# FNet plus MLP on one core: the MLP sums of row blocks 1 and 2 kept in bank layout and added in the last column transform

## The chip, the cores and the metric

The kernel runs on one core of a Trainium2 chip. The metric is device time in microseconds of one execution; for the kernel before it is 849.5 us, the median of three runs (849.11 to 849.95). The engines are named as in the profile: PE (TensorE, matmuls), PEld (its weight loads), DVE (VectorE), ACT (ScalarE), POOL (GpSimd) and SP (SyncE, which here only issues DMAs). An engine works through its own instructions in the order in which the program lists them, and waits for others by semaphores. "us" is microseconds. L189 means line 189 of the kernel before.

## What is computed

The input `x` has 2048 rows of 640 columns. With `xn` the rows of `x` normalised, the output is x plus the real part of a two-dimensional Fourier transform of `xn` plus a two-layer MLP of `xn` with a GELU between. Both parts are matrix products in float32:

```python
a = einsum("bsd,ed->bse", xn, dft_hid_re)
b = einsum("bsd,ed->bse", xn, dft_hid_im)
y = einsum("ts,bse->bte", dft_seq_re, a) - einsum("ts,bse->bte", dft_seq_im, b)
h = gelu(einsum("bsd,df->bsf", xn, w1) + b1)
out = x + y + einsum("bsf,fd->bsd", h, w2) + b2
```

## The kernel before

Each float32 operand of a matmul is split into a high and a low part (`split`, L176): ACT writes the high part (`high`, L186), DVE subtracts it from the operand for the low part (`low`, L189). A product is then three matmuls (`product`, L297 to L302): high by high, high by low, low by high. The rows are worked in four blocks `t` = 0 to 3 of 512 rows (`TB`). PE's results gather in eight PSUM banks of 128 partitions by 512 columns. The 640 output columns of a block are five column blocks `e` of 128. A bank holds one of them "as the matmul leaves it": 128 partitions of columns by 512 rows. To get to the row layout of `x` and of the output, DVE turns 32 by 32 blocks (`nc.vector.transpose`).

**The MLP first.** Its hidden products and output products run over the four row blocks; `oacc[t][e]` is the bank of the sum of block `t` and column block `e`. Block 0 comes first. The calls of `pair(k)` (L1059) then make the hidden units of blocks 1 and 2 together, and the output products of block 1. The last output products of block 1 and those of block 2 run in a loop over `p` = 0 to 13, where one step of PE is 15 matmuls or 3.4 us up to p = 11, with `between(p)` (L1107) as the work beside it. When the sum of a block is complete, each of its five banks is emptied: ACT adds the bias `b2c` in the bank, DVE transposes the bank into an SBUF tile, and DVE adds this to rows of `x` that were loaded for it (`load_xo`, L373). For block 1 these are `turn_sum` and `add_sum` at p = 1 and 4 and `finish` (L953) at p = 4, 5 and 6; for block 2 it is the function `fill` at p = 13. `store_sums` (L973) then writes x plus sum to DRAM, to the three tensors `ys`, split by columns (`YCOLS`: 64, 64 and 32 of the 160 columns that a group of 32 partitions holds). The SBUF tiles in which the transposes land are slots of rings of two: tags `yt`, `ab` and `zt`. The same `zt` slots are used at p = 7 to 9 by the transposes of the normalised rows of block 3 (`transpose_z`, L257). Those rows come by `put_z` (L778), sixteen DMAs issued half on POOL and half on SP at p = 3. `split_unit(g + 2, ...)` at step p prepares the operand `hs` which PE uses in step p + 2.

**The Fourier part after it.** The sequence transform runs first for one half (h = 0) and all four blocks, then for the other (h = 1), block 3 first. Behind blocks 3 and 0 stands one column transform for both (`("y", (3, 0))`), and behind blocks 1 and 2 the last one of the kernel. In it `ta` is 1 and `tb` is 2, and `last` is true. Each of these stages is a scheme of seven products `w` = 0 to 6 in place of eight. In a column transform each product has three entries `u`, so that the last stage has entries n = 0 to 20. `hidden_entry` (L1690) issues an entry's matmuls. They add into the banks named X, Y, Z (two banks each, so one bank past the first is `X + 1`), US and VS; the pairs are taken in the order X, Y, Z, X, Z, X, X for the seven products. The moving operand `as` is a ring of three tiles: behind entry n the kernel makes the operand of entry n + 3 (`form`, L547), with a `high` on ACT and a `low` on DVE, and then runs the work listed for n in `hidden_beside` (L1533, table at L1632). This table is the order in which DVE gets its work in the last stage. `t2`, `t3` and `t4` in it combine the sums `u` and `v` of the two blocks. The rest takes results out of the banks: `to` turns a bank pair and adds it to rows, `odd` does that for the bank US, `copy` moves a bank pair to a sum in SBUF with ACT, `v1` adds the bank pair X to the sum "v1", and `in_two` and `late_rows` turn such sums and add them to rows. `last_columns` turns 32 of each group's columns of block 1's rows into a tile `A["end"]`, and `end(k)` adds that to the last bank.

In the last stage the rows to which everything is added are block 1's `ya = yo[ta]`, loaded by `load_yo` (L1478), and block 2's `columns(0)`, `columns(1)` and `yo[tb, 4]`, loaded by `load_yb` (L1558) and `load_y4` (L1486). Before the change all of these hold x plus the MLP sum, from `ys`. Entry 18 issues fifteen matmuls into VS and fifteen into the first bank of X; entry 19 finishes the two halves of the second bank. After that DVE turns the last results and SP and ACT issue the stores.

Of the kernel before, what the change touches and what calls it, by code (L numbers as in the profile page):

```python
# [15 lines left out]
P = 128  # L16
# [10 lines left out]
def kernel(  # L27
# [72 lines left out]

    YCOLS = ((0, 2 * B), (2 * B, 4 * B), (4 * B, 5 * B))
    ys = [dram.tile([NT, P, NB, c1 - c0], F32, name=f"ys{k}") for k, (c0, c1) in enumerate(YCOLS)]

    GWIDE = (3, 3, 3, 2, 2, 2, 3)
    wits = [dram.tile([ND, P, 2, n * P], F32, name=f"wit{w}") for w, n in enumerate(GWIDE)]
# [867 lines left out]
    def store_sums(t, *ks):  # L973
        for k in ks or range(len(YCOLS)):
            c0, c1 = YCOLS[k]
            nc.gpsimd.dma_start(ys[k][t], xo[t][:, :, c0:c1])

    in_zt = {"home": mr, "tag": "zt"}

    LASTK = NF // 2 - 1  # L980

    def beside_pair(k, at):

        if k == 0:
# [36 lines left out]
        if k == 1:  # L1021
            steps = {7: (0,), 4: (1,)}
        elif k == 2:
            steps = {5: (-1,), 7: (0, 1), 4: (2,)}
        elif k == LASTK:
            steps = {3: (0,), 7: (1, 2)}
        else:
            steps = {3: (0,), 7: (1,), 4: (2,)}
        if at == (7 if k == 1 else 3) and j + 1 < ND:
            load_w(0, j + 1)  # L1030
            load_w(1, j + 1)
        if k == LASTK and at == 3:
            load_x(12)
            load_x(13)
        for n in steps.get(at, ()):
            prep_w(*((j - 1, 2) if n < 0 else (j, n)))
        if k == LASTK and at == 7:
            A["gs"] = place("xab3", (P, 5, TB), F32)
            for i in range(3, 6):
                load_unit(i)  # L1040
        if k == LASTK and at == 2:
            for i in range(3):
                load_unit(i)
        if k == LASTK and at == 4:
            load_x(14)
            load_x(15)
            for i in range(6, 8):
                load_unit(i)
            load_xo(1, place("xab2", (P, NB, DQ), F32))

    units = {}

# [54 lines left out]
    def between(p):  # L1107
# [2 lines left out]
            ln_stats(12)  # L1110
            ln_stats(13)
        if p == 1:
            held = [turn_sum(1, e) for e in (3, 4)]
            A["held"] = held
            ln_stats(14)
        if p == 2:
            ln_stats(15)
        if p == 3:
# [3 lines left out]
                ln_apply(c)  # L1122
            put_z(Z["z"], row_places, nc.gpsimd, nc.sync)
            new_xt(3)
        if p == 4:
            for e, yt in zip((3, 4), A["held"]):
                add_sum(1, e, yt)
        if 4 <= p < 7:
            finish(1, p - 4, home=in_zt)
        for j in {7: (0,), 8: (1, 2), 9: (3, 4)}.get(p, ()):  # L1130
            if j == 0:
                transpose_z("x30", Z["z"], 0)
# [10 lines left out]
        if p in (0, 1, 4, 8):  # L1143
            load_unit({0: 8, 1: 9, 4: 10, 8: 11}[p])
        if p == 10:
            store_sums(1)
            put_rows(3, row_places, nc.sync)
        if p == 12:
            load_xo(2)

    def fourier_step(i):
        if 2 <= i < 2 + 2 * NK:
# [54 lines left out]
    for p in range(2 + NF):  # L1207
# [4 lines left out]
        elif p == NF + 1:  # L1212
# [2 lines left out]

            def fill(k):
                if k == 0:
                    kept[3] = turn_sum(2, 3, rows, "yt")
                else:
                    kept[4] = turn_sum(2, 4, rows, "yt")  # L1220
                    kept[0] = turn_sum(2, 0, **in_zt)
                    kept[1] = turn_sum(2, 1, **in_zt)
                    kept[2] = turn_sum(2, 2)

            kept = {}
            gelu(g + 2, acc, fill)
            for e in (3, 4, 0, 1, 2):
                add_sum(2, e, kept[e])
            store_sums(2)
# [117 lines left out]
    PARTS = slice(0, TB // 2), slice(TB // 2, TB)  # L1347
    X, Y, Z, US, VS = 0, 3, 5, 2, 7
    yo = {}

    def beside(h, t, n):

# [107 lines left out]
        else:  # L1460
# [15 lines left out]
            if n == 6 and p == 2:  # L1476

                def load_yo():  # L1478
                    yo[t] = out_pool.tile([P, NB, DQ], F32, tag="zo", bufs=1, name=f"yo{t}")
                    for k, (c0, c1) in enumerate(YCOLS):  # L1480
                        nc.sync.dma_start(yo[t][:, :, c0:c1], ys[k][t])

                post.append(load_yo)
            if n == 6 and second:

                def load_y4():  # L1486
                    yo[t, 4] = A["y4"](f"y4_{t}")
                    nc.sync.dma_start(yo[t, 4], ys[2][t])

                post.append(load_y4)  # L1490
            if n == 11 and p == 3:
                post += [lambda: open_g(b), lambda: [load_g(b, i) for i in range(3, len(A["g", b]))]]
            if n == 13 and p == 1:
                post += [lambda: open_g(b), lambda: [load_g(b, i) for i in range(3, len(A["g", b]))]]
            if n == 13 and direct:
# [37 lines left out]
    def hidden_beside(b, n):  # L1533
# [22 lines left out]
            return s(1 if last else 0, ("u1", "u2")[k]).rearrange("p a b -> p (a b)").rearrange("p (n e) -> p n e", n=NB)  # L1556

        def load_yb(k):  # L1558
            return lambda: nc.sync.dma_start(columns(k), ys[k][tb])

        def copy(dst, src):
# [50 lines left out]
        def late_rows(h):  # L1612
# [77 lines left out]
    def hidden_entry(n, b, w, u):  # L1690
# [12 lines left out]
        if w == 6 and last:  # L1703

            if u == 0:
                for pos in range(ND):
                    use_g(bank(VS), 2, pos, False, pos == ND - 1)
                for pos in range(ND):
                    wide(0, pos)
            elif u == 1:  # L1710
# [10 lines left out]
        for pos in mine:  # L1721
            if w < 2:
                use_g(bank(US), 2, pos, w == 0 and pos == 0, w == 1 and pos == ND - 1)
            if w == 2:
                use_g(bank(VS), 2, pos, pos == 0, False)
            if w == 6 and u == 2:
                use_g(bank(VS), 2, pos, False, True)
        for pos in mine:
# [78 lines left out]
```

## The time and the profile before

| | |
|---|---|
| median of three runs | 849.5 us |
| lowest and highest run | 849.11 and 849.95 us |
| the profiled execution: first to last instruction (span) | 847.6 us |
| granted TensorE clock, mean | 1.00 |
| the last column transform, first to last matmul | 781.9 to 843.5 us |

The profiled execution gives its span only; the runs' times hold some 2 us more than that span, for what lies before the first and behind the last instruction. The rows of the profile read as follows. A timeline row has the start in us, the length in us, the engine, the line, the operation, what it writes and reads, and in brackets how long the engine was idle ahead of it and what ended that idle time. A row of stretches has, for PE, PEld, DVE, ACT and POOL in turn, the busy us and in parentheses the number of instructions, then the granted clock, the share of time in which the DMA engines were busy, and GB/s. A row of DMA issues has what is written from what, the queue, how many, the size of each, and the median us from issue to landing.

### The profile page before, as it was taken

How to read it: one execution, taken by the hardware profiler on the slowest of the kernel's cores; microseconds unless marked ns; L12 is line 12 of the kernel's file. 1: busy time of each engine (PE TensorE's matmuls, PEld its weight loads, DVE VectorE, ACT ScalarE, POOL GpSimd, SP SyncE). 2: the span in 40 equal slices, each digit the busy share in tenths (PEclk: the TensorE clock that was granted, in tenths of full speed). 3: DMA queues.
4: the chain of work that ended last, by engine and by line, in shares of the span. 5: the costliest groups of instructions: out<-in, count | busy, mean ns of one | idle time of the engine just before them, and what ended most of it. 6: DMA issues, size and time to landing. Idle time of an engine off the chain costs nothing.

```text
span 847.6 us, 10644 instructions
## 1 busy us (share of the span) xinstructions
PE 841.1 (99%) x3725; PEld 696.8 (82%) x3725; DVE 684.3 (81%) x902; ACT 366.1 (43%) x526; POOL 77.8 (9%) x135
## 2 busy tenths in 40 slices
PE   8999999999999999999999999999999999999998
PEld 7888888888888888888888888888888888888886
DVE  5969888767854778979978887899977998886687
ACT  6556657545453555443444343232322433223241
POOL 3340024222301000000000000000000000000012
PEclk9999999999999999999999999999999999999999
DMA  7995767878977897958644679663744799805454
GB/s 223 289 247 160 162 169 244 260 224 299 255 190 205 328 330 143 204 127 188 158 137 108 166 221 287 162 141 99 207 161 152 234 234 230 313 19 180 125 168 111
DMA packets 195332, 166.52 MB, mean 196 GB/s; under 512 B 57648, under 2 KB 166704, under 8 KB 194768
## 3 DMA queue, kind: packets, MB, share of 16 engines
q1 hardware_dynamic: 185216, 139.51, 61.7%
q0 software_dynamic: 7888, 25.83, 9.0%
q10 hardware_dynamic: 2176, 0.52, 0.3%
q8 instruction: 29, 0.48, 0.2%
q14 instruction: 23, 0.19, 0.1%
HBM read 115.75 MB, written 46.14 MB: 191 GB/s over the span
## 4 chain that ended last, share of the span: by engine, by line
PE 99%; ACT 0%; DMA 0%; issue 0%; DVE 0%; SPq 0%
PE banks L302 30%; PE banks L301 30%; PE banks L300 30%; PE banks L320 10%; DMA row<-in_A_x_dram 0%; PE banks L688 0%; ACT xp L721 0%; ACT scratch L715 0%; ACT xp L709 0%; ACT scratch L708 0%; DVE yo L1768 0%; SPq L208 0%; PE banks L742 0%; ACT mv L698 0%
## 5 line engine op out<-in xcount | busy, mean ns | idle before, releaser
L300 PE MATMUL banks<-as,xab 128*128 128x512 f32 (+1 forms) x412 | 159.4, 387 | 0.0
L302 PE MATMUL banks<-as,xab 128*128 128x512 f32 (+1 forms) x412 | 159.4, 387 | 0.0
L301 PE MATMUL banks<-as,xab 128*128 128x512 f32 (+1 forms) x412 | 159.4, 387 | 0.0
L186 ACT ACTIVATE as<-r 128x1024 fp32r<-128x1024 f32 x80 | 85.0, 1062 | 171.2 <-PE banks L302 147.5
L189 DVE TENSOR_TENSOR as<-r,as 128x1024 fp32r<-128x1024 f32 x80 | 97.2, 1216 | 38.1 <-ACT as L186 37.9
L301 PEld LDWEIGHTS banks<-as,xab 128*128 128x128 f32 x412 | 77.4, 188 | 15.7
L300 PEld LDWEIGHTS banks<-as,xab 128*128 128x128 f32 x412 | 77.4, 188 | 15.7
L302 PEld LDWEIGHTS banks<-as,xab 128*128 128x128 f32 x412 | 77.4, 188 | 15.7
L302 PE MATMUL banks<-as,xc 128*128 128x512 f32 x224 | 87.2, 389 | 0.0
L300 PE MATMUL banks<-as,xc 128*128 128x512 f32 x224 | 87.2, 389 | 0.0
L301 PE MATMUL banks<-as,xc 128*128 128x512 f32 x224 | 87.2, 389 | 0.0
L186 ACT ACTIVATE as<-rt 128x1024 fp32r<-128x1024 f32 x32 | 34.0, 1063 | 72.5 <-PE banks L302 57.9
L320 PE MATMUL banks<-xt,xab 128*128 128x512 f32 x240 | 56.7, 390 | 0.0
L320 PEld LDWEIGHTS banks<-xt,xab 128*128 128x128 f32 x240 | 45.0, 188 | 9.3
L1300 POOL DMA_DIRECT2D out_dram<-yo x4 | 2.6, 660 | 518.1 <-DVE yo L463 518.1
L189 DVE TENSOR_TENSOR hs<-ab,hs 128x512 fp32r<-128x512 f32 x36 | 24.7, 687 | 31.1 <-ACT hs L186 30.8
L302 PEld LDWEIGHTS banks<-as,xc 128*128 128x128 f32 x224 | 42.1, 188 | 8.8
L301 PEld LDWEIGHTS banks<-as,xc 128*128 128x128 f32 x224 | 42.1, 188 | 8.7
L300 PEld LDWEIGHTS banks<-as,xc 128*128 128x128 f32 x224 | 42.1, 188 | 8.7
L302 PE MATMUL banks<-hs,xc 128*128 128x512 f32 x120 | 46.7, 390 | 0.0
L300 PE MATMUL banks<-hs,xc 128*128 128x512 f32 x120 | 46.7, 390 | 0.0
L301 PE MATMUL banks<-hs,xc 128*128 128x512 f32 x120 | 46.7, 389 | 0.0
(240 smaller groups left out, 1684.2 us busy)
## 6 DMA issues: line engine op xcount, KB each, us to landing
raw<-in_A_dft_seq_re_dram SPq DMA_DIRECT2D x64, 256.0 KB, 5.5
raw<-in_A_dft_seq_im_dram SPq DMA_DIRECT2D x64, 256.0 KB, 5.0
w1r<-in_B_w_dram SPq DMA_DIRECT2D x144, 80.0 KB, 3.3
wit<-wst POOLq DMA_DIRECT2D x15, 384.0 KB, 4.1
wit<-wst POOLq DMA_DIRECT2D x20, 256.0 KB, 4.3
forms_ab<-xab SPq DMA_DIRECT2D x4, 1280.0 KB, 8.3
xab<-wit SPq DMA_DIRECT2D x13, 384.0 KB, 5.1
row<-xn SPq DMA_DIRECT2D x14, 320.0 KB, 7.0
```

What stands on the lines that cost most here:

```text
L186: nc.scalar.activation(h, s, AF.Copy)
L189: nc.vector.tensor_tensor(l, s, h.bitcast(F32), op=ALU.subtract)
L300: nc.tensor.matmul(acc, wh, mh, start=first, stop=False, skip_group_check=goes_on)
L301: nc.tensor.matmul(acc, wh, ml, start=False, stop=False, skip_group_check=goes_on)
L302: nc.tensor.matmul(acc, wl, mh, start=False, stop=last, skip_group_check=goes_on)
L320: nc.tensor.matmul(acc, W1[i][:, a, j * P : (j + 1) * P], XT[j][:, b], start=n == 0, stop=n == len(steps) - 1)
L1300: queues[q % len(queues)].dma_start(rows_of(out, t)[:, :, q * DQ + c0 : q * DQ + c1], src[q * B : (q + 1) * B])
```

## The change

The banks of blocks 1 and 2 are no longer turned and added to x. A new `keep_sum` adds the bias on ACT while it moves the bank to an SBUF slot, unturned, and POOL writes that to a DRAM tensor `sums_t[t]`. The loads of x rows in this part of the kernel (`load_xo(1)`, `load_xo(2)`), the transposes, the adds and `store_sums` for these blocks go. For block 0 `ys` stays as it was.

In the last stage the rows of blocks 1 and 2 are now loaded from `x` itself, in pieces of a group of 32 partitions each (`load_columns`, and `load_yo`). The kept sums are loaded by six POOL DMAs at the end of the last sequence transform (`load_sums`), into two places whose last use by PE is there. They are added in bank layout, by adds on DVE in the table of `hidden_beside`: to bank pair X on the way to SBUF at entry 3, the pair Y at entry 6, US for both blocks at entry 7, Z and X in place of two copies on ACT at entries 9 and 12, VS in place at entry 10, `A["end"]` at entry 11, and the first bank of X in place at entry 17. At entry 3 a transpose and an add go, since X and Y are turned together. The flags of PE's accumulation into VS change with the add into that bank; the matmuls are the same in number, shape and order.

```diff
+    sums_t = {t: dram.tile([P, ND, TB], F32, name=f"sums_t{t}") for t in (1, 2)}
...
+    def keep_sum(t, e, home=mr, tag="ab", name="ks"):
+
+        kept = home.tile([P, TB], F32, tag=tag, bufs=2, name=f"{name}{t}_{e}")
+        nc.scalar.activation(kept, oacc[t][e], AF.Identity, bias=b2c[:, e : e + 1])
+        nc.gpsimd.dma_start(sums_t[t][:, e], kept)
...
-            load_xo(1, place("xab2", (P, NB, DQ), F32))
...
         if p == 1:
-            held = [turn_sum(1, e) for e in (3, 4)]
-            A["held"] = held
+            for e in (3, 4):
+                keep_sum(1, e)
...
-        if p == 4:
-            for e, yt in zip((3, 4), A["held"]):
-                add_sum(1, e, yt)
         if 4 <= p < 7:
-            finish(1, p - 4, home=in_zt)
+            keep_sum(1, p - 4, **in_zt)
...
         if p == 10:
-            store_sums(1)
             put_rows(3, row_places, nc.sync)
-        if p == 12:
-            load_xo(2)
...
+    def load_columns(dst, t, c0, c1):
+        for q in range(Q):
+            nc.sync.dma_start(dst[q * B : (q + 1) * B], rows_of(x, t)[:, :, q * DQ + c0 : q * DQ + c1])
+
+    def load_sums(ta, tb):
+        a, b = (place(f"xc{n}{n + 1}", (P, 7, TB), F32) for n in (0, 2))
...
+        for dst, t, e0, e1 in ((a, ta, 0, 2), (a, ta, 4, 5), (b, tb, 4, 5), (b, tb, 2, 4), (b, tb, 0, 2), (a, ta, 2, 4)):
+            nc.gpsimd.dma_start(dst[:, e0:e1], sums_t[t][:, e0:e1])
...
+            if n == 13 and p == 3:
+                post.append(lambda: load_sums(blocks[b - 1][1], t))
...
         def load_yb(k):
+            if last:
+                return lambda: load_columns(columns(k), tb, *YCOLS[k])
...
+        sa, sb = A["sums"] if last else (None, None)
+        both = sa[:, 5:7] if last else None
+
+        def first_two():
+            add(both, both, y_)
+            to(ya[:, :, : 2 * B], both, f"ya2_{ta}", out_a(0, 2 * B))()
+
         def odd():
+            if last:
+                add(sa[:, 4], sa[:, 4], us)
+                add(sb[:, 4], sb[:, 4], us)
+                add_turned(ya[:, :, 4 * B :], turned(sa[:, 4], f"yo_{tb}"))
+                out_a(4 * B, DQ)()
+                return
...
-            3: [to(ya[:, :, : 2 * B], x_, f"ya1_{ta}")],
+            3: [lambda: add(both, x_, sa[:, 0:2])] if last else [to(ya[:, :, : 2 * B], x_, f"ya1_{ta}")],
...
-            6: [to(ya[:, :, : 2 * B], y_, f"ya2_{ta}", out_a(0, 2 * B)), t2(2)],
+            6: [first_two if last else to(ya[:, :, : 2 * B], y_, f"ya2_{ta}"), t2(2)],
...
-            9: [copy(s(1, "v1"), z_), t3(1)],
-            10: [t3(2)],
-            11: [t4(0)],
-            12: [copy(s(1, "v2"), x_), t4(1)],
+            9: [lambda: add(s(1, "v1"), z_, sb[:, 2:4]) if last else copy(s(1, "v1"), z_)(), t3(1)],
+            10: [t3(2)] + ([lambda: add(vs, vs, sb[:, 4])] if last else []),
+            11: [t4(0)] + ([lambda: add(A["end"], A["end"], sa[:, 3])] if last else []),
+            12: [lambda: add(s(1, "v2"), x_, sb[:, 0:2]) if last else copy(s(1, "v2"), x_)(), t4(1)],
...
-            17: [v1, *late_rows(0)] if last else [yb1, yb2],
+            17: [v1, lambda: add(bank(X), bank(X), sa[:, 2]), *late_rows(0)] if last else [yb1, yb2],
```

More of the change, by code (lines that the diff above doesn't have):

```diff
@@ L1217, in fill @@
                 if k == 0:
-                    kept[3] = turn_sum(2, 3, rows, "yt")
+                    keep_sum(2, 3, rows, "yt")
                 else:
[L1220 to L1225, printed above, removed]
+                    keep_sum(2, 4, rows, "yt")
+                    keep_sum(2, 0, **in_zt)
+                    keep_sum(2, 1, **in_zt)
+                    keep_sum(2, 2)
             gelu(g + 2, acc, fill)
-            for e in (3, 4, 0, 1, 2):
-                add_sum(2, e, kept[e])
-            store_sums(2)
         else:
@@ L1349 @@
     yo = {}
+    def load_columns(dst, t, c0, c1):
[3 more added lines that the diff above has]
+        a, b = (place(f"xc{n}{n + 1}", (P, 7, TB), F32) for n in (0, 2))
+        A["sums"] = a, b
+        for dst, t, e0, e1 in ((a, ta, 0, 2), (a, ta, 4, 5), (b, tb, 4, 5), (b, tb, 2, 4), (b, tb, 0, 2), (a, ta, 2, 4)):
+            nc.gpsimd.dma_start(dst[:, e0:e1], sums_t[t][:, e0:e1])
     def beside(h, t, n):
@@ L1479, in load_yo @@
                     yo[t] = out_pool.tile([P, NB, DQ], F32, tag="zo", bufs=1, name=f"yo{t}")
-                    for k, (c0, c1) in enumerate(YCOLS):
-                        nc.sync.dma_start(yo[t][:, :, c0:c1], ys[k][t])
+                    for q in range(Q):
+                        nc.sync.dma_start(yo[t][q * B : (q + 1) * B], rows_of(x, t)[:, :, q * DQ : (q + 1) * DQ])
                 post.append(load_yo)
@@ L1487, in load_y4 @@
                     yo[t, 4] = A["y4"](f"y4_{t}")
-                    nc.sync.dma_start(yo[t, 4], ys[2][t])
+                    if p == 3:
+                        load_columns(yo[t, 4], t, 4 * B, DQ)
+                    else:
+                        nc.sync.dma_start(yo[t, 4], ys[2][t])
                 post.append(load_y4)
@@ L1706, in hidden_entry @@
                 for pos in range(ND):
-                    use_g(bank(VS), 2, pos, False, pos == ND - 1)
+                    use_g(bank(VS), 2, pos, False, pos == ND - 1, True)
                 for pos in range(ND):
@@ L1724, in hidden_entry @@
             if w == 2:
-                use_g(bank(VS), 2, pos, pos == 0, False)
+                use_g(bank(VS), 2, pos, pos == 0, last and pos == ND - 1)
             if w == 6 and u == 2:
```

## The prediction

> **What bounds the kernel now.** I read the page's engine line first, then the table of who waited for whom with the rows of PE, then stretches of the last stage.
>
> ```profile
> span 847.6 us, 10644 instructions
> PE 841.1 (99%) x3725; PEld 696.8 (82%) x3725; DVE 684.3 (81%) x902; ACT 366.1 (43%) x526; POOL 77.8 (9%) x135
> ```
>
> ```profile
> PE banks L672 <- POOL warm L660: 2.0, 1, 2.0
> PE banks L688 <- ACT xp L721: 0.4, 1, 0.4
> ```
>
> TensorE (PE) is busy from end to end. Its only two waits in the whole span are before its first real product. The change neither adds nor removes a matmul, so in the body nothing can get shorter: work taken off VectorE (DVE), ScalarE (ACT) and the queues comes off engines for which PE never waits. The time can only grow, where an engine that now runs just ahead of PE falls behind it, or shrink in the few us after the last matmul. So the question is who has how much lead, and where the change puts its work. It puts it in the last stage, the column transform of row blocks 1 and 2 (781.9 to 843.5).
>
> ```profile
> 782.00:807.70 25.70, 25.70 (x115) 21.30 (x114) 14.65 (x15) 6.57 (x7) 0.00 (x0) 1.00 0.38 112
> 807.70:836.40 28.70, 28.70 (x128) 23.71 (x128) 27.40 (x29) 11.68 (x13) 5.18 (x8) 1.00 0.48 143
> 843.60:847.60 4.00, 0.00 (x0) 0.00 (x0) 0.40 (x1) 0.00 (x0) 0.00 (x0) 1.00 0.59 131
> ```
>
> These are stretches with the busy time of PE, PEld, DVE, ACT and POOL, then the granted clock. In the first 25.7 us DVE works 14.65; in the next 28.7 us it works 27.40. There it has 1.3 us to spare, and that is where six of the seven added operations land (the seventh, at entry 17, comes as that stretch ends). DVE's queue there, some rows left out:
>
> ```profile
> 807.73 1.23 DVE L189 TENSOR_TENSOR as<-u,as 128x1024 fp32r<-128x1024 f32 x1 [2.07 <-ACT as L186]
> 808.87 1.24 DVE L1322 STREAM_TRANSPOSE ya<-banks 128x1024 f32<-128x1024 f32 x1
> 810.15 1.23 DVE L463 TENSOR_TENSOR yo<-yo,ya 128x1024 f32<-128x1024 f32 x1
> ...
> 813.03 0.71 DVE L1319 STREAM_TRANSPOSE yo<-banks 128x512 f32<-128x512 f32 x1
> 813.77 0.69 DVE L463 TENSOR_TENSOR yo<-yo,yo 128x512 f32<-128x512 f32 x1
> 814.38 0.69 DVE L463 TENSOR_TENSOR y<-y,yo 128x512 f32<-128x512 f32 x1
> 814.98 0.68 DVE L189 TENSOR_TENSOR as<-u,as 128x512 fp32r<-128x512 f32 x1
> ...
> 816.72 1.22 DVE L189 TENSOR_TENSOR as<-v,as 128x1024 fp32r<-128x1024 f32 x1
> 817.86 1.22 DVE L463 TENSOR_TENSOR u<-u,u 128x1024 f32<-128x1024 f32 x1
> 819.98 1.23 DVE L189 TENSOR_TENSOR as<-v,as 128x1024 fp32r<-128x1024 f32 x1 [0.90 <-ACT as L186]
> ...
> 824.59 1.22 DVE L463 TENSOR_TENSOR v<-v,u 128x1024 f32<-128x1024 f32 x1
> 826.04 1.23 DVE L189 TENSOR_TENSOR as<-u,as 128x1024 fp32r<-128x1024 f32 x1 [0.23 <-ACT as L186]
> ...
> 828.39 1.22 DVE L463 TENSOR_TENSOR v<-v,banks 128x1024 f32<-128x1024 f32 x1
> 829.64 1.25 DVE L1322 STREAM_TRANSPOSE yb<-v 128x1024 f32<-128x1024 f32 x1
> ...
> 834.78 1.22 DVE L463 TENSOR_TENSOR v<-v,banks 128x1024 f32<-128x1024 f32 x1
> 836.03 0.71 DVE L1618 STREAM_TRANSPOSE yb<-v 128x512 f32<-128x512 f32 x1
> ```
>
> Read the start times. An operation of 1024 columns takes its successor 1.13 us later (816.72 to 817.86), one of 512 columns 0.60 (814.38 to 814.98), and a 1024 add whose result the next one reads 1.25 (828.39 to 829.64). From 807.73 to 836.03 the queue stops only at 819.98 and 826.04.
>
> **The prices, part by part.** I count places by the entries 0 to 20 of the stage (three to each of its seven products w; entries 18 to 20 are the last product).
>
> *Ahead of 807.73.* Entry 3 loses a transpose and an add of 1024 columns into `ya` and gets one add: about 1.2 us less DVE work. But DVE then waits 2.07 us for ACT ahead of 807.73, so this is worth nothing.
>
> *From 807.73 on.* Entry 6: one more 1024 add whose result is transposed next, +1.25. Entry 7: two adds, a transpose and an add for a transpose and two adds, +0.60. Entry 9: a 1024 add on DVE in place of a copy on ACT, +1.13. Entry 10: 512 add into bank VS, +0.60. Entry 11: 512 add into `end`, +0.60. Entry 12: a 1024 add for an ACT copy, +1.13. Entry 17: a 512 add into bank X behind `v1`, +0.60. Sum **5.91 us**.
>
> *What comes back.* The two stops. The first ends 0.99 us after the queue could have gone on (819.98 against 817.86 + 1.13), the second 0.32 (826.04 against 824.59 + 1.13). Both wait for ACT:
>
> ```profile
> 817.97 1.03 ACT L1562 ACTIVATE v<-banks 128x1024 f32<-128x1024 f32 x1 [1.42 <-DVE as L189]
> 818.90 1.57 ACT L186 ACTIVATE as<-v 128x1024 fp32r<-128x1024 f32 x2
> ```
>
> The copy L1562 that stands ahead of the first of these goes, and a DVE that is two us late finds both operands there. So 1.31 comes back, and the add into bank X ends at 836.00 + 5.91 - 1.31 = **840.60**.
>
> *When PE wants it.* Bank X is added to by the last product, which in PE's order comes after 15 matmuls into VS:
>
> ```profile
> 819.31 0.39 PE L300 MATMUL banks<-as,ws 128*128 128x512 f32 x1
> ...
> 826.11 0.39 PE L300 MATMUL banks<-as,gr_a 128*128 128x512 f32 x1
> ...
> 836.36 0.39 PE L300 MATMUL banks<-as,xab 128*128 128x512 f32 x1
> ...
> 843.24 0.28 PE L302 MATMUL banks<-as,xab 128*128 128x256 f32 x1
> 843.55 0.45 DVE L1768 STREAM_TRANSPOSE yo<-banks 128x256 f32<-128x256 f32 x1 [0.81 <-PE banks L302]
> ```
>
> The three L300 rows are the first matmuls of products 4 and 5 and of bank X in product 6. Today `v1`, which reads X, ends at 836.00 and X is written from 836.36. After, X can start at 840.65, allowing 0.05 for the signal: **4.29 us late**. PE loses them on the way, in holds that nest and don't add. Product 4 writes bank Z, which the new add of entry 9 reads: by the same count that add ends near 820.97 against 819.31, a hold of 1.7. Product 5 writes X behind the add of entry 12 (about 829.0; PE then due at 827.8): another 1.2. The rest falls on the last operands `as` (L189) and on bank X. Behind 836.36 the order of work is the same; DVE's last piece has 0.81 us of idle ahead of it and stays shifted with PE. So the last matmul, the last transpose (843.55) and the stores move by the same 4.3, and what lies beyond the last matmul does not change.
>
> *Unseen operations, bounded.* The new adds have forms that the rows show (SBUF with PSUM into SBUF, and PSUM with SBUF into PSUM), so I bound each by 0 to 10% off. [...]
>
> *The DMA side.* The x columns now come as eight small SP DMAs in place of two, the sums as six on POOL at the stage's start, where POOL has nothing else queued.
>
> ```profile
> u<-ys SPq DMA_DIRECT2D x4, 512.0 KB, 4.0
> out_dram<-u SPq DMA_DIRECT2D x8, 128.0 KB, 3.0
> gs<-zc POOLq DMA_DIRECT2D x6, 256.0 KB, 3.9
> ys<-xab POOLq DMA_DIRECT2D x1, 256.0 KB, 6.6
> forms_c<-xc SPq DMA_DIRECT2D x4, 896.0 KB, 10.7
> ```
>
> The first x columns can start when t4(0) is done (about 826.1 with DVE's lateness by then), and DVE wants them about 835.9. Four DMAs of 128 KB like the stores above, issued over some 2 us and landing 3.0 later, are there by 831: hidden by 5 us. The slowest row, 10.7, would make them 2.5 us late. The sums are wanted from 798.7 on and can be asked for from 779: hidden even at 10.7.
>
> *The middle (204 to 256).* Bias, transpose and add of ten blocks become an ACT operation and a POOL DMA each. DVE gets lighter, and PSUM banks come free after ACT alone. But a slot of tag `zt` is now freed by a DMA:
>
> ```profile
> 215.82 4.38 POOL L782 DMA_DIRECT2D z<-row  x8 [13.06 <-DVE row L231]
> 220.97 0.64 ACT L382 ACTIVATE banks<-banks,b2c 128x512 f32<-128x512 f32 x1
> 230.17 0.69 DVE L189 TENSOR_TENSOR hs<-g,hs 128x512 fp32r<-128x512 f32 x1
> ```
>
> The first kept sum of block 1 queues on POOL behind `put_z` until 220.2. Landing after 3.9, it holds the third (now at 220.97) to 224.1; that one lands about 228.6, and the transposes of `z` (the second waits for that slot) and `hs` (now 230.17) behind it slip by some 1 us. PE wants that `hs` at 233.8, two outputs later: cost nothing. At 6.6 both steps slip and `hs` is ready near 236.9: 3 us. I take nothing, by the `gs` row, which has the same shape.
>
> **Sum.** 847.6 + 4.3 = 851.9 us of span. The runs' median is 849.5, 1.9 above this span, for what lies around it; it is carried over: **853.8 us**.
>
> **The rivals.**
> (a) *DVE takes over the last stage*, as summed: 853.8, own range 852.8 to 855.0 (prices 10% either way are 0.6; the rest is signals). For it: 1.3 us to spare against 5.9 added. Chance 0.72.
> (b) *The same, and a DMA is late as well*: in the `zt` slots or the x columns, up to 3 us: 854.5 to 857. Against it: the landings of the nearest rows. Chance 0.14.
> (c) *Not slower.* DVE absorbs it all: PE is held only if the additions exceed 1.31 us of stops plus 0.3 of lead on bank X. For that they would have to cost 1.6 and not 5.9, which could be if DVE's back-to-back rows, like 829.64 behind 828.39, are spaced by their producers, so that independent adds fit between them. Against it: rows with no dependence keep 1.13 too (816.72, 817.86). Time 849.5; chance 0.08 for no change. For a gain, the lighter queues would have to bring the stores behind 843.5 in sooner, at most 4.1 us of span: 847.5, chance 0.04.
> (d) *The clock.* If holds of PE cost the granted clock and it is halved from bank X to the end (836.36 to 843.5), 7.2 us more: 861. Against it: the row 843.60:847.60 grants 1.00 over 4.0 us without a matmul. Chance 0.02. [...]
>
> **How the numbers follow.** Within 0.2% of the median (1.7 us, about what a measurement of this kernel can tell from no change) counts as the same. Faster 0.04, same 0.08, slower 0.88. The range reaches from below (a)'s own range into (b), 852.3 to 857.0; outside it lie (c), (d) and the edges of (b), under 0.2.
>
> **What would show it.** After: DVE without a stop from about 808 to 842; waits of PE for DVE on L463 and L189, absent today, of 4 us together, the first near 819 at product 4, the last ahead of bank X; the same 4.1 us from the last matmul to the end; and no wait of PE before 819. Wrong: PE holds between 210 and 260 (then (b)), a DVE that idles in the last 30 us waiting for a DMA (b), or PE still without waits, (c).

## The result: 855.9 us, 0.7% slower

The changed kernel takes 855.88 us, the median of four executions (855.01 to 856.80), against 849.52 for the kernel before: a ratio of 1.007, with a 95% interval of 1.0056 to 1.0084. That is 6.4 us more, where 4.3 were forecast. The profiled execution took 856.67 us, with a span of 854.9.

The page's engine line and the table of who waited for whom, of the changed kernel:

```profile
span 854.9 us, 10669 instructions
PE 843.1 (99%) x3725; PEld 696.8 (82%) x3725; DVE 677.6 (79%) x888; ACT 364.4 (43%) x524; POOL 79.6 (9%) x145
```

```profile
PE banks L302 <- ACT as L188: 2.7, 2, 1.7
PE banks L674 <- POOL warm L662: 2.0, 1, 2.0
PE banks L303 <- DVE as L191: 1.7, 2, 1.2
PE banks L302 <- DVE banks L465: 0.4, 1, 0.4
PE banks L690 <- ACT xp L730: 0.2, 1, 0.2
```

DVE is busy for less time than before (677.6 against 684.3 us) and has fewer instructions, ACT too, and the kernel is slower. PE has five waits that it did not have. The rows of PE with an idle time ahead of them show where they are (L188 and L191 are the lines `high` and `low` after the change, L465 is `add`):

```profile
351.34 0.50 PE L303 MATMUL banks<-as,xab 128*128 128x512 f32 x1 [1.20 <-DVE as L191]
...
822.96 0.47 PE L302 MATMUL banks<-as,ws 128*128 128x512 f32 x1 [1.67 <-ACT as L188]
...
831.04 0.47 PE L302 MATMUL banks<-as,gr_a 128*128 128x512 f32 x1 [0.99 <-ACT as L188]
...
840.25 0.50 PE L303 MATMUL banks<-as,xab 128*128 128x512 f32 x1 [0.52 <-DVE as L191]
...
842.72 0.50 PE L302 MATMUL banks<-as,xab 128*128 128x512 f32 x1 [0.36 <-DVE banks L465]
```

Four of the five are in the last stage, at product 4, product 5, the last operands, and bank X. Two of those are put down to ACT, which is a case of the releaser named being the wrong one of several. DVE's and ACT's rows ahead of the first:

```profile
819.25 1.22 DVE L465 TENSOR_TENSOR u<-u,u 128x1024 f32<-128x1024 f32 x1
820.39 1.22 DVE L191 TENSOR_TENSOR as<-v,as 128x1024 fp32r<-128x1024 f32 x1
821.64 1.23 DVE L465 TENSOR_TENSOR v<-banks,xc 128x1024 f32<-128x1024 f32 x1
...
829.72 1.22 DVE L465 TENSOR_TENSOR v<-banks,xc 128x1024 f32<-128x1024 f32 x1
```

The adds of entries 9 and 12 read Z and X (`v<-banks,xc`) and end at 822.87 and 830.94. PE goes on 0.09 and 0.10 later, at 822.96 and 831.04. It is the bank that PE waits for, and DVE that is late.

The profiled execution had a fifth hold, at 350 us, far from anything that the prediction looked at. Up to 340 us its matmuls run 0.33 us later than those of the kernel before, behind the hold 1.82, so the hold cost 1.5 us; the shortest executions (855.0) are 1.7 shorter than this one. To separate the parts, two DVE rows serve as marks in every kernel: the `low` that has 2.07 us of idle ahead of it (807.73 before), where DVE's crowded stretch begins, and the last transpose (843.55 before). The changed kernel was profiled a second time (the run e8_again below), and that execution had no hold at 350 us:

| | crowded stretch begins | last transpose | between them | span | last transpose to end |
|---|---|---|---|---|---|
| before | 807.73 | 843.55 | 35.82 | 847.6 | 4.05 |
| after | 809.55 | 850.04 | 40.49 | 854.9 | 4.86 |
| after, second profile | 807.83 | 848.33 | 40.50 | 853.2 | 4.87 |

```profile
809.55 1.23 DVE L191 TENSOR_TENSOR as<-u,as 128x1024 fp32r<-128x1024 f32 x1 [2.07 <-ACT as L188]
...
850.04 0.45 DVE L1795 STREAM_TRANSPOSE yo<-banks 128x256 f32<-128x256 f32 x1 [0.77 <-PE banks L304]
```

So the loss has three parts: **4.7 us** in the last stage, in both profiles; **0.8 us** behind the last transpose, in both; and between 0.1 and 1.8 us ahead of the last stage, most of which comes and goes.

### The profile page after: what moved, and what is told of

Same layout as the page of the kernel before. It is cut to its first block, busy times and chain, and to the rows that moved or that the text cites. A ratio compares the mean times of both kernels' runs of the same rounds, so it can differ in the third digit from the quotient of the medians.

```text
span 854.9 us, 10669 instructions
## 1 busy us (share of the span) xinstructions
PE 843.1 (99%) x3725; PEld 696.8 (82%) x3725; DVE 677.6 (79%) x888; ACT 364.4 (43%) x524; POOL 79.6 (9%) x145
## 4 chain that ended last, share of the span: by engine, by line
PE 93%; DVE 5%; issue 1%; ACT 1%; DMA 0%; POOL 0%; SPq 0%; DVEq 0%; ACTq 0%
PE banks L303 28%; PE banks L302 28%; PE banks L304 28%; PE banks L322 10%; DVE as L191 2%; DVE v L465 1%; DVE u L465 1%; DMA row<-in_A_x_dram 0%; DVE rt L465 0%; ACT as L188 0%; DVE rt L526 0%; DVE xc L465 0%; DVE r L465 0%; DVE yo L465 0%; PE banks L690 0%
## 5 line engine op out<-in xcount | busy, mean ns | idle before, releaser
L188 ACT ACTIVATE as<-r 128x1024 fp32r<-128x1024 f32 x80 | 85.0, 1062 | 171.1 <-PE banks L304 150.4
L191 DVE TENSOR_TENSOR as<-r,as 128x1024 fp32r<-128x1024 f32 x80 | 97.1, 1215 | 37.9 <-ACT as L188 37.8
L188 ACT ACTIVATE as<-rt 128x1024 fp32r<-128x1024 f32 x32 | 34.0, 1063 | 72.5 <-PE banks L304 57.9
L191 DVE TENSOR_TENSOR hs<-ab,hs 128x512 fp32r<-128x512 f32 x36 | 24.8, 688 | 42.4 <-ACT hs L188 42.1
L1356 POOL DMA_DIRECT2D xc<-sums_t x6 | 3.2, 545 | 486.2 <-PE banks L304 484.6
```

Of the source, the lines that this page charges most:

```text
L188: nc.scalar.activation(h, s, AF.Copy)
L191: nc.vector.tensor_tensor(l, s, h.bitcast(F32), op=ALU.subtract)
L1356: nc.gpsimd.dma_start(dst[:, e0:e1], sums_t[t][:, e0:e1])
```

## The experiments

Two theories were set against each other. **A**: the seven adds on DVE make the last stage late, as the prediction says. **B**: the new middle (banks kept unturned) or the new loads set the time.

### The adds alone, taken out and put in

The first kernel is the changed one without the adds and with the two ACT copies back. The adds are nine instructions; one, at entry 3, took the place of a transpose and an add, and from entry 6 on they are, counted net, the prediction's seven. Three places of the edit:

```diff
-            3: [lambda: add(both, x_, sa[:, 0:2])] if last else [to(ya[:, :, : 2 * B], x_, f"ya1_{ta}")],
+            3: [to(ya[:, :, : 2 * B], x_, f"ya1_{ta}")],
...
-            9: [lambda: add(s(1, "v1"), z_, sb[:, 2:4]) if last else copy(s(1, "v1"), z_)(), t3(1)],
+            9: [copy(s(1, "v1"), z_), t3(1)],
...
-            17: [v1, lambda: add(bank(X), bank(X), sa[:, 2]), *late_rows(0)] if last else [yb1, yb2],
+            17: [v1, *late_rows(0)] if last else [yb1, yb2],
```

> The changed kernel without the seven adds of the last stage (entries 3, 6, 7, 9, 10, 11, 12 and 17 as in the kernel before, the two ACT copies of v1 and v2 back); sums are still kept and loaded, and the MLP sums of row blocks 1 and 2 are left out of the output. Theory A (the adds on DVE make the last stage late): the holds of PE at 821, 830, 840 and 842 us of the changed kernel go, the last stage is that of the kernel before, and the time is 849.5 to 850.5, or some 1.5 us more in an execution that has the hold at 350 us. Rival B (the new middle or the loads of sums and x set the time): it stays at 855.

The second has the middle of the kernel before and only the changed table of the last stage, with zeros in place of the loaded sums:

```diff
+        for dst in (a, b):
+            nc.gpsimd.memset(dst[:, 0:5], 0.0)
```

> The middle of the kernel before (sums turned, added to rows and stored there) with the seven adds of the last stage on tiles of zeros, that POOL fills in place of the loads. Theory A: the last stage is late by about 4.5 us all the same, 854.0 to 854.5, and no execution has the hold at 350 us if that hold comes from the new middle. Rival B: 849.5.

Measured: without the adds 850.26 us (850.03 to 851.15, ratio 1.0009, interval 1.0000 to 1.0018); the adds alone 854.76 (854.57 to 856.18, ratio 1.0065, interval 1.0051 to 1.0078). The table of who waited for whom without the adds has one line, the wait for `warm` that the kernel before has too:

```profile
PE banks L674 <- POOL warm L662: 2.0, 1, 2.0
```

With the adds alone it has the waits of the changed kernel again, less the one at 350 us (line numbers are lower by one there):

```profile
PE banks L301 <- ACT as L187: 2.7, 2, 1.7
PE banks L673 <- POOL warm L661: 2.0, 1, 2.0
PE banks L302 <- DVE as L190: 0.5, 1, 0.5
PE banks L301 <- DVE banks L464: 0.4, 1, 0.4
```

And its two marks, then those of the kernel without the adds:

```profile
807.88 1.23 DVE L190 TENSOR_TENSOR as<-u,as 128x1024 fp32r<-128x1024 f32 x1 [2.07 <-ACT as L187]
...
848.38 0.45 DVE L1800 STREAM_TRANSPOSE yo<-banks 128x256 f32<-128x256 f32 x1 [0.77 <-PE banks L303]
```

```profile
807.65 1.23 DVE L191 TENSOR_TENSOR as<-u,as 128x1024 fp32r<-128x1024 f32 x1 [2.07 <-ACT as L188]
...
843.45 0.45 DVE L1789 STREAM_TRANSPOSE yo<-banks 128x256 f32<-128x256 f32 x1 [0.78 <-PE banks L304]
```

With the adds alone they are 40.50 us apart, 4.68 more than before, to a hundredth what the changed kernel shows. Without the adds they are 35.80 apart, as before (35.82). The last stage's loss is the adds', all of it; theory B has no share in it. The kernel without the adds is still some 0.7 us over the kernel before, and that is the longer end: 848.3 - 843.45 = 4.85 us behind its last transpose.

### Three of the seven left out

Entries 10, 11 and 17 lose their adds of 512 columns; the rest stays:

```diff
-            10: [t3(2)] + ([lambda: add(vs, vs, sb[:, 4])] if last else []),
-            11: [t4(0)] + ([lambda: add(A["end"], A["end"], sa[:, 3])] if last else []),
+            10: [t3(2)],
+            11: [t4(0)],
...
-            17: [v1, lambda: add(bank(X), bank(X), sa[:, 2]), *late_rows(0)] if last else [yb1, yb2],
+            17: [v1, *late_rows(0)] if last else [yb1, yb2],
```

> The changed kernel without the adds of entries 10, 11 and 17 (three of the seven; their parts of the sums are left out of the output). Theory A counts DVE's queue end to end: of 4.2 us, 2.5 stay, so 853.2 beside 855.0 of the changed kernel (854.9 in an execution with the hold at 350 us). A rival by which the hold follows from something other than the length of DVE's queue (the two copies moved off ACT alone): 855, no change, since entries 9 and 12 stay.

Measured: 853.30 us (853.02 to 853.92, ratio 1.0044, interval 1.0031 to 1.0057). Its waits:

```profile
PE banks L674 <- POOL warm L662: 2.0, 1, 2.0
PE banks L302 <- ACT as L188: 1.7, 1, 1.7
PE banks L303 <- DVE as L191: 0.5, 1, 0.5
```

The hold of product 4 stands as it was, because no add ahead of entry 9 was removed; those of product 5 and bank X are gone. The marks are 846.34 - 807.66 = 38.68 apart: 2.86 us more than before, where the count gave 2.5 and the changed kernel has 4.68. The three adds were priced at 3 x 0.60 = 1.8 us, and 40.50 - 38.68 = 1.82 came back. So the holds follow the length of DVE's queue. The two ACT copies are missing here as well, so their loss alone does not set them.

### The hold at 350 us

In the profile of the changed kernel, DVE at 315 us waits for rows of the Fourier input that land late, and PE waits for DVE when the next stage begins at 350:

```profile
315.40 0.42 DVE L465 TENSOR_TENSOR sums<-row 128x256 f32<-128x256 f32 x1 [0.34 <-DMA row<-xn]
...
317.65 0.42 DVE L465 TENSOR_TENSOR sums<-row,sums 128x256 f32<-128x256 f32 x1 [1.13 <-DMA row<-xn]
```

Issues of `row<-xn` in the stretch from 300 to 318 us took 12.0 us to land. In the second profile the same issues took 9.4, in the kernel before 9.9. DVE carries the delay on to the next stage: its `low` (L191) that PE waits for starts at 350.08, where the kernel before has it at 348.05. One kernel laid the new DRAM tiles out last, so that all others keep their old addresses; another was the changed kernel again:

```diff
-    sums_t = {t: dram.tile([P, ND, TB], F32, name=f"sums_t{t}") for t in (1, 2)}
...
+    sums_t = {t: dram.tile([P, ND, TB], F32, name=f"sums_t{t}") for t in (1, 2)}
```

> The changed kernel with the new DRAM tiles of the sums laid out behind all others, so that the others keep the addresses that they have in the kernel before. If the hold at 350 us came with the shifted addresses: no execution has it and all lie at 855.0. If it comes from the new middle or by chance: some executions at 855.0 and some at 856.7, as the changed kernel had.

> The changed kernel once more, for the share of its executions that have the hold at 350 us. If the hold is tied to the change: most of the executions at 856.7. If it is chance: the executions spread from 855.0 to 856.8, as two and two did at first.

Measured: 855.26 (855.10 to 855.85) and 855.46 (854.99 to 855.72). Neither has an execution at 856.7, so of the changed kernel's nine executions two are there and the other seven spread from 855.0 to 855.7. The kernel with the old middle and the adds alone has one at 856.18 among four from 854.57 to 855.00, and that one was not profiled. Old addresses don't remove the spread: e3_sums_last has two of its five executions 0.59 and 0.75 us above the fastest. The profile of its slowest has no hold at 350 us; it is 1.0 us late already at 345 us, 0.3 of it by a delay behind 78.95 us. So the hold at 350 is one of several places where an execution can lose time ahead of the last stage. What makes the rows land late in some executions stays open. It is not needed for the 4.7 or the 0.8 us.

### The longer end

Behind its last issue SP runs nine waits one after the other, among them those for the last stores (from 844.91 to 846.73 us in the kernel before, by the trace's records of semaphores). The kernel before has 592 issues on SP, the changed one 594. If the place of the last store among these waits moves with the number of issues, it can come early, and the other waits stand behind it. Two kernels test that. The kernel before gets two more issues by splitting loads in halves, and the changed kernel six more:

```diff
+                        if k < 2:
+                            for h in (0, NB // 2):
+                                nc.sync.dma_start(yo[t][:, h : h + NB // 2, c0:c1], ys[k][t, :, h : h + NB // 2])
...
```

> The kernel before with two of SP's loads of sums split in halves, so that SP issues 594 transfers in place of 592, as in the changed kernel; nothing else differs. Theory T (the 0.8 us behind the last transpose come from the order in which SP waits for its queues' last transfers at the end of the program, and this order moves with the number of transfers that SP issued): the end takes 4.8 in place of 4.1 us, and the time is 850.2 to 850.4. Rival: the longer end comes with the new loads or stores, or with the length of the code: 849.5, no change.

```diff
-                    for q in range(Q):
-                        nc.sync.dma_start(yo[t][q * B : (q + 1) * B], rows_of(x, t)[:, :, q * DQ : (q + 1) * DQ])
+                    for q, w in enumerate((NB // 4, NB // 4, NB, NB)):
+                        for h in range(0, NB, w):
+                            nc.sync.dma_start(yo[t][q * B : (q + 1) * B, h : h + w], rows_of(x, t)[:, h : h + w, q * DQ : (q + 1) * DQ])
```

> The changed kernel with SP's first load of x columns in ten parts in place of four, so that SP issues 600 transfers, as many modulo 8 as the 592 of the kernel before. Theory T: the end behind the last transpose takes 4.1 us again and the fastest executions are at 854.3 in place of 855.0. Rival: 855.0, no change.

Measured: 849.96 (849.64 to 850.45, ratio 1.0003, interval 0.9994 to 1.0012) and 855.01 (854.67 to 855.39). The first is under the expected range and can't be told from no change by its time; the second is 0.45 us under the changed kernel beside it, its fastest execution 0.3 (854.67 against 854.99) where 0.7 was expected. The last transpose of the first, whose span is 848.1 us, and of the second, whose span is 852.9:

```profile
843.69 0.45 DVE L1772 STREAM_TRANSPOSE yo<-banks 128x256 f32<-128x256 f32 x1 [0.75 <-PE banks L302]
```

```profile
848.40 0.45 DVE L1796 STREAM_TRANSPOSE yo<-banks 128x256 f32<-128x256 f32 x1 [0.77 <-PE banks L304]
```

The kernel before with two issues more has an end of 4.41 in place of 4.05; the changed one with six more 4.50 in place of 4.87. Each moved in the expected direction, by half of what was expected. The kernel with the adds alone has 592 issues and an end of 852.8 - 848.38 = 4.42, which seems to speak against the theory. The records of landings split the end in two:

| | issues on SP | last transpose to last landing | last landing to end |
|---|---|---|---|
| before | 592 | 3.10 | 0.97 |
| adds alone (e2_last_alone) | 592 | 3.45 | 0.96 |
| before, two issues more (e6_two_dmas) | 594 | 3.10 | 1.34 |
| changed, six issues more (e7_six_dmas) | 600 | 3.16 | 1.33 |
| changed, both profiles | 594 | 3.08 | 1.78 |
| before, two idle POOL adds (e10_pool_alone, below) | 592 | 3.10 | 1.19 |

With the adds alone only the last store landed later; behind it the end is that of the kernel before. With 592 and 600 issues the store that lands last is waited for in the eighth of SP's nine waits, with 594 in the second, and the seven waits behind it follow at 0.06 us each. Six waits more are 0.37 us, in e6_two_dmas and in the changed kernel alike: this half is the order of the waits. The other half, 0.44 us, is a stop behind the waits. In the changed kernel SP's next instruction comes 0.36 us after its last wait, in place of 0.06, and itself takes 0.13 us in place of 0.01; with six issues more POOL goes on 0.39 us behind SP, in place of 0.03. The five other kernels with the new loads and 594 issues have the same 1.78. What stops SP and POOL there stays open, and so does the 0.2 us that e10_pool_alone has over the kernel before.

### The sums added earlier

The plan (sums unturned, x by itself) does not force the adds into the crowded stretch. Ahead of 807.73 DVE works 14.65 of 25.7 us. In the next kernel the sums of block 1 and one part of block 2 are turned there on DVE and added to the rows of x, some adds by POOL; v1 and v2 are ACT copies as before, and POOL adds their sums to them:

```diff
+        def early(src, e0, e1, spare, dst, eng):
+            w = spare[:, 5 : 5 + e1 - e0]
+
+            def f():
+                nc.vector.transpose(w.rearrange("p e n -> p (e n)"), src[:, e0:e1].rearrange("p e n -> p (e n)"))
+                d = dst.rearrange("p n (e i) -> p e n i", i=B)
+                eng.tensor_tensor(d, d, w.rearrange("p e (n i) -> p e n i", i=B), op=ALU.add)
+
+            return f
+
+        def beside_sums(k, part):
+            return lambda: nc.gpsimd.tensor_tensor(s(1, k), s(1, k), part, op=ALU.add)
...
+            9: [copy(s(1, "v1"), z_)] + ([beside_sums("v1", sb[:, 2:4])] if last else []) + [t3(1)],
```

> The same plan, sums kept unturned and x loaded by itself, with the sums added elsewhere: they are turned on DVE before 807 us, where it stands idle, and added to the rows by POOL and DVE; v1 and v2 are ACT copies again and POOL adds their sums to them in SBUF. Theory A (the loss is the place of the adds in DVE's queue, not the plan): no hold of PE after 815 us, 849.8 to 851, with the longer end that the run without the adds had. Rival: turning and adding the sums anywhere in this pair is too much, and POOL's adds to v1 and v2 come too late for their splits: holds of 1 to 3 us, 851.5 to 854.

Measured: 854.71 us (854.40 to 855.18, ratio 1.0060, interval 1.0047 to 1.0072). Theory A's number missed, and the rival's range is passed too. In the trace the longest hold of PE (1.30 us, at 829.07) is put down to a `low` on DVE, and DVE's operations beside POOL's adds are the long ones (first POOL, then DVE; the two of the crowded stretch):

```profile
819.85 2.40 POOL L1604 TENSOR_TENSOR v<-v,xc 128x1024 f32<-128x1024 f32 x1 [1.69 <-ACT v L1576]
824.93 3.00 POOL L1604 TENSOR_TENSOR v<-v,xc 128x1024 f32<-128x1024 f32 x1 [2.68 <-ACT v L1576]
```

```profile
820.75 2.59 DVE L191 TENSOR_TENSOR as<-v,as 128x1024 fp32r<-128x1024 f32 x1 [0.90 <-ACT as L188]
...
825.60 3.41 DVE L191 TENSOR_TENSOR as<-u,as 128x1024 fp32r<-128x1024 f32 x1
```

These two DVE operations are `low`s that take 1.22 us elsewhere. They end at 823.34 and 829.01; POOL's adds end at 822.25 and 827.93. Each DVE operation ends 1.1 us behind POOL's add, as if it had stood still until POOL was done and then taken about its usual time. Two kernels test that. In one, all adds are on DVE and none on POOL, and at entries 9 and 12 a DVE add again takes the place of the ACT copy. In the other, the kernel before gets two POOL adds whose results nobody reads (on tiles that POOL fills with zeros at the stage's start; the add at entry 12 is not shown):

```diff
+        def alone(k, c):
+            return [lambda: nc.gpsimd.tensor_tensor(sb[:, c : c + 2], s(1, k), sa[:, c : c + 2], op=ALU.add)] if last else []
...
-            9: [copy(s(1, "v1"), z_), t3(1)],
+            9: [copy(s(1, "v1"), z_)] + alone("v1", 0) + [t3(1)],
...
```

> The version with the sums added early, once more, with every add on DVE and none on POOL: the three early adds that POOL had, and v1 and v2 read from their banks with the sums in one DVE add each, as in the changed kernel. Theory P (the early version lost its time because DVE's adds of two tiles in SBUF stand while POOL adds): DVE laid end to end gives 1.2 us of lateness from the two adds at entries 9 and 12, and with the longer end of 0.8 us this makes 851.3 to 851.8; no DVE add of 128x1024 takes over 1.3 us. Rival Q (turning and adding the sums in this pair is too much work wherever it is put): 854 to 855 as before.

> The kernel before, with two adds of 128x1024 on POOL beside it whose results nobody reads, each behind the ACT copy of v1 or v2; the result is complete. Theory P: the DVE add beside each takes 2.4 to 3.4 in place of 1.22 us, PE is held by some 1 to 3 us in all, 850.8 to 852.5. Rival Q (POOL and DVE do not hinder each other, and the early version lost its time to POOL's lateness alone): DVE's adds stay at 1.22 us and the time at 849.6.

Measured: all adds on DVE 851.99 us (851.60 to 852.68, ratio 1.0023, interval 1.0013 to 1.0033); POOL's two idle adds beside the kernel before 853.92 (853.37 to 854.63, ratio 1.0048, interval 1.0036 to 1.0060). In the latter, POOL and then DVE:

```profile
819.67 2.40 POOL L1587 TENSOR_TENSOR xc<-v,xc 128x1024 f32<-128x1024 f32 x1 [1.76 <-ACT v L1570]
824.80 2.93 POOL L1587 TENSOR_TENSOR xc<-v,xc 128x1024 f32<-128x1024 f32 x1 [2.74 <-ACT v L1570]
```

```profile
820.50 2.65 DVE L189 TENSOR_TENSOR as<-v,as 128x1024 fp32r<-128x1024 f32 x1 [0.90 <-ACT as L186]
...
824.27 1.21 DVE L463 TENSOR_TENSOR v<-v,u 128x1024 f32<-128x1024 f32 x1
825.41 3.41 DVE L189 TENSOR_TENSOR as<-u,as 128x1024 fp32r<-128x1024 f32 x1
```

DVE ends at 823.15 and 828.82, again 1.1 us behind POOL's 822.07 and 827.73. The kernel with two POOL adds whose results nobody reads takes 4.3 us more (853.92 against 849.63 beside it), where 1 to 3 were expected. 3.2 of them are in the last stage, whose marks are 847.29 - 808.25 = 39.04 apart; 0.5 was there already when the stage began (its first matmul is at 782.43, before at 781.91), ahead of POOL's adds. Rival Q is out in both its forms, and so is the reading that theory A had failed: with POOL out of the way the early version comes within 0.2 us of the range expected of it. What the traces show is this: a DVE operation on two SBUF tiles that started during POOL's add of two SBUF tiles ended 1.1 us behind it, in all four cases above. The other direction shows too: POOL's second add started inside a DVE add of two SBUF tiles (824.27 to 825.48) and took 2.93 in place of 2.40. A DVE transpose out of the banks was not held in the one case there is: in e5_early it ran from 809.59 to 810.82, beside a POOL add from 808.63 to 810.81, and took 1.23 us, where the kernel before has 1.24 (at 808.87).

With all adds on DVE the same plan takes 3.5 us less than the changed kernel did when it was run again (855.46), and no DVE operation of that stretch takes over 1.25 us. It still takes 2.4 us more than the kernel before (849.63 beside it): the two adds at entries 9 and 12 remain in the crowded stretch (its last transpose is at 845.33, 1.8 late, of which 0.3 was there when the stage began (782.19 against 781.91) and 1.5 came in the stage, where 1.2 were expected), and it has the longer end (850.2 - 845.33 = 4.87). No version was found that beats the kernel before.

## Why the prediction was right, and where it was short

**Direction and mechanism: right.** Slower was given 0.88, and the time lies in the range (852.3 to 857.0), 2.1 us above the forecast. It is just past the end of case (a)'s own range (855.0), inside (b)'s, though nothing was late in the two places that (b) names. Of the 2.1 us, 0.4 came in the last stage, 0.8 behind the last transpose, and the rest ahead of the last stage, where the forecast had nothing: that the time lies in the range is in part luck.

**"Worth nothing" ahead of 807.73: right.** Entry 3's saving is not to be found: the `low` behind it has the same 2.07 us of idle ahead of it in all profiles of the changed kernel.

**5.91 added, 1.31 back, 4.29 late at bank X: right to 0.4.** In the second profile of the changed kernel, which started the crowded stretch only 0.10 us later than the kernel before, the rows read:

```profile
807.83 1.22 DVE L191 TENSOR_TENSOR as<-u,as 128x1024 fp32r<-128x1024 f32 x1 [2.07 <-ACT as L188]
808.98 1.21 DVE L465 TENSOR_TENSOR xc<-xc,banks 128x1024 f32<-128x1024 f32 x1
...
818.66 1.22 DVE L191 TENSOR_TENSOR as<-v,as 128x1024 fp32r<-128x1024 f32 x1
819.92 1.22 DVE L465 TENSOR_TENSOR v<-banks,xc 128x1024 f32<-128x1024 f32 x1
821.06 1.22 DVE L465 TENSOR_TENSOR u<-u,u 128x1024 f32<-128x1024 f32 x1
...
839.00 1.22 DVE L465 TENSOR_TENSOR v<-v,banks 128x1024 f32<-128x1024 f32 x1
840.24 0.70 DVE L465 TENSOR_TENSOR banks<-banks,xc 128x512 f32<-128x512 f32 x1
...
848.33 0.45 DVE L1795 STREAM_TRANSPOSE yo<-banks 128x256 f32<-128x256 f32 x1 [0.77 <-PE banks L304]
```

The add into bank X ends at 840.94, less the 0.10 at 840.84, where the count gave 840.60. Two spacings of 1.13 are in fact wider: 1.26 ahead of the add of entry 9 (818.66 to 819.92) and 1.24 ahead of the add into bank X (839.00 to 840.24). That is the 0.24. The new adds themselves took 1.22 and 0.70, what the rows of before said; an add that reads a bank (`v<-banks,xc`) and one of two SBUF tiles (`u<-u,u`) both took 1.22. The matmul that waits for the add into bank X starts 0.06 later, at 841.00; the 0.05 that the forecast allows for the signal was an estimate. From bank X's start to the last transpose it took 848.33 - 841.00 = 7.33 us where it took 7.19 before:

```profile
841.00 0.50 PE L302 MATMUL banks<-as,xab 128*128 128x512 f32 x1 [0.36 <-DVE banks L465]
841.34 0.39 PE L303 MATMUL banks<-as,xab 128*128 128x512 f32 x1
841.57 0.39 PE L304 MATMUL banks<-as,xab 128*128 128x512 f32 x1
```

That is 0.14 more. 4.29 + 0.24 + 0.14 make 4.67, and 4.68 was measured.

**The holds and their order: right.** Predicted were 1.7 at product 4 near 819 and 1.2 at product 5, then the last operands, then bank X. The idle times are 1.67, 0.99, 0.52 and 0.36, in that order, 3.5 us together. Counted from one matmul's start to the next the four holds cost 4.2, since a row's 0.39 us reaches past the usual next start (0.23 later), and the matmul behind each comes some 0.1 late. So they add up to nearly all of the 4.7. DVE has no stop from 809.55 to the 0.77 us ahead of its last transpose in the changed kernel's first profile.

**"What lies beyond the last matmul does not change": wrong, by 0.8 us.** This is the step that failed. The stores are the same, and the last of their data is through 2.95 us behind the start of the last matmul (2.96 before); but the end behind the last transpose grew from 4.05 to 4.85 us or more in every profile of a kernel with the new loads and 594 issues on SP. Of this 0.37 us is the place of the last store among SP's final waits, which moved with the number of its issues; 0.44 is a stop of SP behind these waits, whose cause stays open. The prediction took "the same stores" to mean the same end and put nothing for either.

**The DMA side and the middle: right for what they were asked.** The x columns landed in 2.7 us in the median, the sums in 4.4 and 3.5, and no DVE instruction of the last stage waits for them. PE has no wait between 200 and 262 us, so the `zt` slots cost nothing, and (b) is not what happened there.

```profile
xc<-sums_t POOLq DMA_DIRECT2D x4, 512.0 KB, 4.4
...
u<-in_A_x_dram SPq DMA_DIRECT2D x8, 128.0 KB, 2.7
xc<-sums_t POOLq DMA_DIRECT2D x2, 256.0 KB, 3.5
```

**"No wait of PE before 819": wrong in some executions.** The hold at 350 us follows a DMA that lands late, as in (b), in a place that (b) did not name. It is in the changed kernel's first profile and not in its second.

**(c) and (d) fell.** The spacing of DVE's independent adds is real: leaving out three shortened the stage by 1.8 us. The granted clock stayed at 1.00 through all four holds of the last stage, and no run shows it halved: the executions' means are 0.998 to 1.000.

```profile
807.70:836.40 28.70, 26.04 (x114) 20.91 (x114) 26.68 (x29) 9.32 (x10) 2.61 (x4) 1.00 0.52 141
836.40:850.00 13.60, 12.72 (x68) 10.31 (x66) 12.59 (x18) 1.70 (x2) 5.14 (x8) 1.00 0.40 99
```

## What to carry to other kernels

An engine's share of the whole span says little about moving work to it: here DVE got 6.7 us of busy time less and the kernel 6.4 us more, because the work went from stretches where DVE stands idle into the one where it had 1.3 us to spare. Lay the receiving engine's queue end to end over the stretch that gets the work, with spacings read from neighbouring rows, and compare with when the bound engine wants each result; that gave 4.3 of the stage's 4.7 us. Before such work is given to POOL instead, look at what DVE reads beside it: two POOL adds cost 3.2 us of the stage, where they were to save DVE 2.3 (two spacings of 1.13).

## What the runs showed of the hardware

- A DVE operation on two SBUF tiles that started during a POOL add of two SBUF tiles took 2.59 to 3.41 us in the crowded stretch, in place of 1.22, and in all four cases (e5_early, e10_pool_alone) ended 1.1 us behind POOL's add.
- After each hold PE is a little slow at first: in the second profile the matmuls after 841.00 start 0.34 and then 0.23 us apart. Ahead of its first hold six starts, from 818.05 to 819.18, lie 0.226 apart. It adds about 0.1 us to each hold, at a granted clock of 1.00.
- The end of the program is not constant: from the last store's landing to the end 0.96 to 1.78 us with the same stores. 0.37 of this is the place of that store among SP's final waits, at 0.06 us a wait, and it moved with the number of transfers that SP had issued.
